# A relaid start: first key cast ahead of the bias table, first query copy on VectorE alone, other spare matmuls, new queue orders

## The chip, the core and the metric

The kernel runs on one core of one Trainium2 chip. The metric is the device time of one execution in microseconds (us), lower is better. PE is TensorE, DVE is VectorE, ACT is ScalarE, POOL is GpSimd, SP is SyncE.

## What is computed

Attention with a relative-position bias over 8 batches and 8 heads, sequence 576, head size 64, followed by a two-layer feed-forward part over 4608 tokens (512 to 2048 to 512):

```python
scores = scale * np.matmul(q, k.transpose(0, 1, 3, 2))
bias = bias_table[bucket]                 # bucket from |i - j|, 32 buckets
scores = scores + bias.transpose(2, 0, 1)[None, :, :, :]
attn = np.exp(scores - max); attn = attn / attn.sum(-1)
out = np.matmul(attn, v)                  # -> x of 4608 x 512
h = x @ w_in;  g = np.maximum(0.01 * h, h);  return g @ w_out
```

Inputs and output are float32; the kernel multiplies in bfloat16.

## The kernel before

The 64 heads are taken as 32 pairs n = 0 to 31, four pairs to a batch. For a pair, queries and keys stand with 96 rows and are turned on PE (`turn_by_pe`, L488 and L493) for the early pairs, by DMA for the later ones; `take_turned` (L502) copies a turned half from PSUM to SBUF, `apart` (L506) makes a copy with the last 64 columns set apart. `score` gives six units u of scores (L527, L531, L534 and L535), each goes through one exponential on ACT (`expo`, L554, L556, L561). The bias is a factor on the exponentials: DVE's `band` (L578) multiplies a band of them by `hk`, which holds exp(bias difference) by distance. Then `av` (L607, L610) multiplies by the values, `norm` divides, and the result is turned into `xT` (L639). The feed-forward part (`ffn_in` L658, `in_product` L706, `product` L783) takes blocks of 512 tokens and runs between the attention of later pairs; it is there from about 34 us to the end.

Before that stands the start-up. The first pair's keys come by an early DMA as float32 into a piece of `y` (called `raw`), and `raw_rows` (L463) casts them to bfloat16 into `pr`, one half on ACT and one on DVE. The first pair's queries come by a POOL DMA. `hk` is made from the 32 x 8 bias table: `some_runs` and `small_runs` (L373, L385, L386) write a one-hot map of distances, `shift_hot` (L394) repeats it shifted, `shift_table` (L399 to L401) turns the table, subtracts its last row and turns it back, `exp_table` (L406) takes exponentials, `spread` (L414, six times) multiplies map by exponentials on PE, `take_spread` (L417) copies that into `hk`, `make_hk4` (L421) copies parts of it. POOL issues all large loads; `clear_v` and `clear_edges` (L325 to L333) are its memsets.

The order of the work on each engine is written out by hand. Every piece is a task with a number, given in the order in which the program adds it; `Plan.QUEUES` lists the numbers for SP, PE, ACT, DVE and POOL, `BANKS` gives the PSUM banks in PE's order, and a copy that either engine can do (`take_turned`, `x_copy`, `in_take`, `out_take`) runs on the engine whose list holds it. `FILL` names PE tasks ahead of which some spare matmuls of constants are put (256 columns, L1284, results unused), and `spin(19)` puts 19 of them ahead of everything.

Of the kernel before, what the change touches and what calls it, by code (L numbers as in the profile page):

```python
# [36 lines left out]
class Plan:  # L37
# [6 lines left out]
            285 335 261 341 393 990 321 399 349 448 989 454 506 376 407 512 561 434 1051 567 462 1050 619 489 520 674  # L44
            625 1156 575 1155 547 602 680 633 660 730 688 732 1257 715 1256 777 738 827 779 765 829 1358 1357 874 785
            835 812 876 1459 882 1458 862 909 1560 1559 1661 1660 1769 1770 1771 1772 1774""",
        "PE": """
# [27 lines left out]
            1749 1744 1754 1755 1752 1753 1757 1758 1763 1764 1765""",  # L75
        "ACT": """
# [17 lines left out]
            1698 1679 1718 1652 1731 1708 1725 1730 1713 1732 1714 1715 1716 1733 1740 1655 1750 1756 1759 1773""",  # L94
        "DVE": """
# [96 lines left out]
def kernel(  # L192
# [10 lines left out]
    nc = tc.nc  # L203
# [57 lines left out]
    RQ = 96  # L261
# [553 lines left out]
    def dma(at):  # L815
        return add("DMA0", 0.0, [], None, 0, at=at)

    L["raw", 0], L["raw", 1], tabl = dma(4.8), dma(3.85), dma(3.0)
    sh = add("DVE", 0.4, [tabl], shift_table, -99)
    e8t = add("ACT", 0.7, [sh], exp_table, -99)  # L820
    hott, shifts = [], []
# [496 lines left out]
```

## Time and profile before

| | |
|---|---|
| median of three runs | 350.75 us (350.03 to 352.52) |
| the profiled execution, own time | 351.14 us |
| its span in the profile | 349.3 us |
| PE, DVE, ACT, POOL busy | 98%, 86%, 82%, 26% of the span |
| exponentials on ACT at L554 | 124, 1033 ns each |
| spare matmuls (L1284) | 34, the last at 23.8 us |

The execution's time is 1.84 us above its span: that lies outside what the engines' records cover. Rows are read as: start, duration (us), engine, line, operation, tiles, shape, count; a bracket gives the idle time of the engine just ahead and what ended it. Overlapping instructions of one row are counted together, so a row's duration can be shorter than the sum of its instructions.

### The profile page before, as it was taken

The page shows a single profiled execution, that of the slowest core. Times are in us where ns is not written, and L with a number is a line of the kernel's source. Part 1 is how long each engine was busy: PE and PEld are TensorE (multiplying, and loading weights), DVE is VectorE, ACT ScalarE, POOL GpSimd, SP SyncE. Part 2 cuts the span into 40 slices and gives each one's busy share as a digit, 9 for nine tenths or more (in the row PEclk, how much of TensorE's full clock was granted, in tenths as well). Part 3 has the DMA queues.
Part 4 walks back from the last instruction along what each step waited for, and adds up shares of the span by engine and source line. Part 5 has one row for each costly group of instructions (what it writes and reads, how often), then busy time and mean ns, then how long its engine had stood idle before and what let it go on. Part 6 is the DMA issues. An engine that isn't in the chain of part 4 may idle for free.

```text
span 349.3 us, 10523 instructions
## 1 busy us (share of the span) xinstructions
PE 343.7 (98%) x4417; PEld 264.5 (76%) x4428; DVE 300.6 (86%) x644; ACT 285.7 (82%) x444; POOL 91.4 (26%) x131
## 2 busy tenths in 40 slices
PE   8999999999999999999999999999999999999996
PEld 5667457774577787778777877787877888888885
DVE  5899399779899999999999989699989995788853
ACT  6899887689889999989989998889968973686641
POOL 8946223053005600794049403200000000000000
PEclk9999999999999999999999999999999999999999
DMA  8999999969959997999569947913940230110033
GB/s 122 153 188 182 197 197 151 132 77 159 172 132 119 141 186 165 73 88 116 178 83 130 121 108 132 127 38 97 152 36 3 85 94 3 75 48 2 0 122 120
DMA packets 118431, 39.32 MB, mean 113 GB/s; under 512 B 100849, under 2 KB 113265, under 8 KB 118385
## 3 DMA queue, kind: packets, MB, share of 16 engines
q0 software_dynamic: 69168, 18.21, 60.0%
q1 hardware_dynamic: 48864, 20.10, 30.2%
q8 instruction: 34, 0.56, 0.7%
q10 hardware_dynamic: 352, 0.36, 0.4%
q14 instruction: 13, 0.10, 0.1%
HBM read 36.70 MB, written 9.44 MB: 132 GB/s over the span
## 4 chain that ended last, share of the span: by engine, by line
PE 95%; DVE 2%; ACT 1%; DMA 1%; issue 0%; DVEq 0%
PE ps L783 32%; PE ps L706 25%; PE ps L607 12%; PE ps L527 10%; PE ps L658 8%; PE ps L534 2%; PE ps L594 1%; PE ps L547 1%; PE ps L493 1%; PE ps L488 1%; PE ps L414 1%; DMA tab<-in_bias_table_dram 1%; PE ps L639 1%; ACT at L554 1%; PE ps L535 0%
## 5 line engine op out<-in xcount | busy, mean ns | idle before, releaser
L554 ACT ACTIVATE at<-ps 128x1024 bf16<-128x1024 f32 x124 | 123.8, 1033 | 15.4 <-PE ps L527 12.7
L783 PEld LDWEIGHTS <-g 128*128 128x128 bf16 x768 | 72.2, 98 | 14.4 <-issue 3.3
L578 DVE TENSOR_TENSOR at<-at,hk 128x768 bf16<-128x768 bf16 (+4 forms) x156 | 65.7, 448 | 10.4 <-ACT at L554 7.0
L313 POOL DMA_DIRECT2D vn<-in_v_dram x32 | 29.7, 940 | 114.4 <-PE ps L607 82.9
L716 DVE TENSOR_TENSOR stage<-ps,stage 128x512 f32<-128x512 f32 x84 | 55.9, 684 | 4.0 <-PE ps L706 1.9
L783 PE MATMUL ps<-mix,g 128*128 128x256 bf16 x384 | 48.2, 273 | 0.0
L706 PEld LDWEIGHTS <-w_in_sb 128*128 128x128 bf16 x448 | 42.4, 98 | 7.5 <-issue 2.4
L783 PE MATMUL ps<-w_out_sb,g 128*128 128x256 bf16 x384 | 47.7, 273 | 0.0
L607 PE MATMUL ps<-vn,at 128*128 128x65 bf16 x1240 | 45.8, 194 | 0.0
L607 PEld LDWEIGHTS <-at 128*128 128x128 bf16 x1240 | 42.2, 97 | 4.6 <-issue 1.7
L647 ACT ACTIVATE g<-stage 128x512 bf16<-128x512 f32 x72 | 42.8, 641 | 1.9 <-DVE stage L716 1.7
L527 PE MATMUL ps<-qkt 64*128 64x512 bf16 x256 | 42.6, 390 | 0.0
L711 ACT COPY stage<-ps 128x512 f32<-128x512 f32 x56 | 31.4, 594 | 12.3 <-PE ps L706 11.2
L706 PEld LDWEIGHTS <-early 128*128 128x128 bf16 x336 | 31.8, 98 | 5.1 <-issue 0.9
L647 ACT ACTIVATE g<-ps 128x512 bf16<-128x512 f32 x56 | 31.7, 608 | 1.4 <-PE ps L658 0.8
L706 PE MATMUL ps<-early,w_in_sb 128*128 128x256 bf16 x224 | 31.2, 273 | 0.0
L706 PE MATMUL ps<-early 128*128 128x256 bf16 x224 | 30.7, 273 | 0.0
L706 PE MATMUL ps<-xT,w_in_sb 128*128 128x256 bf16 x224 | 29.9, 273 | 0.0
L658 PE MATMUL ps<-xT,w_in_sb 128*128 128x512 bf16 x121 | 29.3, 379 | 0.6 <-issue 0.3
L791 ACT COPY y<-ps 128x512 f32<-128x512 f32 x26 | 15.3, 589 | 14.1 <-PE ps L783 12.4
L796 DVE TENSOR_TENSOR y<-ps,y 128x512 f32<-128x512 f32 (+2 forms) x31 | 18.8, 616 | 7.0 <-ACT y L791 4.0
L625 DVE TENSOR_TENSOR opair<-ps,rcp 128x640 bf16<-128x640 f32 x28 | 23.1, 825 | 1.0
(114 smaller groups left out, 494.8 us busy)
## 6 DMA issues: line engine op xcount, KB each, us to landing
out_dram<-y SPq DMA_DIRECT2D x16, 512.0 KB, 3.6
vn<-in_v_dram POOLq DMA_DIRECT2D x32, 128.0 KB, 6.3
qkn<-in_q_dram POOLq DMA_DIRECT2D x10, 288.0 KB, 8.2
qkn<-in_k_dram POOLq DMA_DIRECT2D x10, 288.0 KB, 8.0
w_in_sb<-in_moe_w_in_dram POOLq DMA_DIRECT2D x2, 1024.0 KB, 11.8
w_out_sb<-in_moe_w_out_dram POOLq DMA_DIRECT2D x2, 1024.0 KB, 17.2
qkn<-in_q_dram POOLq DMA_DIRECT2D x16, 72.0 KB, 4.2
qkn<-in_k_dram POOLq DMA_DIRECT2D x16, 72.0 KB, 4.1
```

The source lines that it names most:

```text
L313: nc.gpsimd.dma_start(out=vn[i][:, c, :, 0:D], in_=v[b, :, c * P : (c + 1) * P, :].rearrange("h s d -> s h d"),)
L527: nc.tensor.matmul(ps[:, e, :], lhsT=kt[r, u * P : (u + 1) * P], rhs=qt[r, 0:512], start=True, stop=True)
L554: nc.scalar.activation(at[:, :, u, 0:512], ps, AF.Exp, scale=scale)
L578: nc.vector.tensor_tensor(out=o, in0=o, in1=m, op=ALU.mult)
L607: nc.tensor.matmul(ps[:, ic, :], lhsT=at[:, o : o + P], rhs=vn[i][:, c, 2 * p + e, :], start=whole and c == 0, stop=not whole and ic == NJ ...
L625: nc.vector.tensor_tensor(out=opairs[n % NOP].rearrange("p i (e d) -> p e i d", e=2), in0=ps[:, :, :, 0:D], in1=rcp.to_broadcast([P, 2, NJ ...
L647: nc.scalar.activation(out_, in_, AF.Prelu, bias=0.0, scale=1.0, alpha=0.01)
L658: nc.tensor.matmul(bank(("in", T, f))[:, o : o + n], lhsT=w_in_sb[:, c, f * P : (f + 1) * P], rhs=xT[:, c, x : x + n], start=(c == 0 and i ...
L706: nc.tensor.matmul(ps[:, j, :], lhsT=l, rhs=r, start=first and j == 0 and c == 0, stop=k in (2, 4, 3) and j == 1 and c == KH - 1, skip_gro ...
L711: copy(out=stage[u % 2][:, s], in_=ps)
L716: nc.vector.tensor_tensor(out=st, in0=ps, in1=st, op=ALU.add)
L783: nc.tensor.matmul(ps, lhsT=l[:, ts * P : (ts + 1) * P], rhs=r[:, cols], start=k in (1, 2, 5) and (split or ts == 0) and j == 0, stop=k in ...
```

## The change

Five things are changed.

1. In DVE's list, `small_runs` and `raw_rows` (the key half) stand ahead of `some_runs(2)` and `shift_table`; before, `shift_table` and `small_runs` came first.
2. The first pair's turned queries are copied by one `take_turned` of 576 columns on DVE. Before, ACT copied the first 288 columns and DVE then the other 288. `take_turned` loses its argument `half`. With that ACT copy, one task (number 25) is gone, so every later number is one lower in the new lists.
3. Spare matmuls: 17 instead of 19 ahead of all, and 13 instead of 15 within; five of them now stand ahead of the first `score`.
4. All five lists and the banks are written anew; in PE's list 147 of 662 tasks keep their place, and some 40 copies change between ACT and DVE, about as many each way. In POOL's list `clear_edges` moves from behind the second `clear_v` to just behind the first values' load, that is ahead of the loads of batch 1's queries and keys and of the first half of `w_in`. In SP's list `x_dma(6)` moves ahead of `turn_by_dma(10)`, and others shift by a place.
5. The planner's own guesses (a landing time, a cost) change, which has no effect on the program by itself.

The first tasks on PE and ACT by name (pair n, unit u or half j; j = 1 keys, 0 queries):

```
PE before:  turn(0,k) turn(0,q) spread4 spread5 score(0,1) spread2 score(0,0) spread1 turn(1,k) turn(1,q)
            score(0,2) spread0 score(0,3) turn(2,q) turn(2,k) score(1,1) spread3 score(0,5) [2 spare] score(0,4) ...
PE after:   turn(0,k) turn(0,q) [5 spare] score(0,3) score(0,2) spread5 spread3 spread4 score(0,0) spread1 score(0,1)
            turn(1,k) turn(1,q) score(0,5) spread0 turn(2,q) score(1,1) spread2 score(1,3) turn(2,k) score(1,2)
            score(1,5) [1 spare] score(1,0) [4 spare] turn(3,k) score(0,4) ...
ACT before: some_runs(1) raw_rows exp_table shift_hot(3) take(0,k) take(0,q, half) expo(0,1) expo(0,0) take(1,k) ...
ACT after:  some_runs(1) raw_rows shift_hot(3) take(0,k) exp_table expo(0,3) expo(0,2) expo(0,0) expo(0,1) take(1,q) ...
DVE before: some_runs(0) some_runs(3) shift_table small_runs raw_rows some_runs(2) shift_hot x2 take(0,q, half)
            take_spread4 5 2 1 take(1,q) take_spread0 ...
DVE after:  some_runs(0) some_runs(3) small_runs raw_rows some_runs(2) shift_table shift_hot x2 take(0,q)
            apart x2 take_spread5 4 3 1 take(1,k) apart take_spread0 take(2,q) take_spread2 make_hk4 x2 ...
```

```diff
     QUEUES = {
         "PE": """
-            24 23 41 43 49 37 47 35 71 70 51 33 53 99 100 78 39 57 55 107 80 129 82 86 128 84 113 111 76 109 64 66 105
+            24 23 52 50 42 38 40 46 34 48 70 69 56 32 98 77 36 81 99 79 85 75 128 54 108 112 83 127 110 106 104 65 63
...
         "ACT": """
-            3 22 1 32 27 25 50 48 73 52 54 79 58 56 108 81 83 85 87 114 112 110 77 106 141 139 116 173 137 143 167 145
+            3 22 31 26 1 53 51 47 49 71 57 78 82 80 76 86 55 109 113 84 111 107 105 140 138 115 165 136 134 166 142 144
...
         "DVE": """
-            2 5 0 6 21 4 31 30 26 42 44 38 36 72 34 75 101 28 29 102 40 46 104 74 45 103 131 132 61 90 130 63 59 60 62
+            2 5 6 21 4 0 30 29 25 27 28 43 41 39 35 72 73 33 100 37 44 45 101 60 102 58 62 103 74 130 59 61 91 129 88 89
...
         "POOL": """
-            7 8 9 10 11 13 14 15 12 16 17 18 19 20 273 274 275 388 389 390 501 502 503 614 615 616 727 728 729 824 825
+            7 8 9 10 11 12 13 14 15 16 17 18 19 20 272 273 274 387 388 389 500 501 502 613 614 615 726 727 728 823 824
...
-    FILL = {55: 2, 86: 3, 128: 2, 113: 2, 111: 1, 76: 1, 109: 1, 64: 2, 140: 1}
+    FILL = {52: 5, 75: 1, 128: 4, 112: 1, 110: 1, 104: 1}
...
-    def take_turned(n, j, copy, half=None):
+    def take_turned(n, j, copy):
...
-        rs = slice(0, RQ) if half is None else slice(half * RQ // 2, (half + 1) * RQ // 2)
-        copy(out=turned_to(n, j).rearrange("p (r c) -> p r c", c=NC)[:, rs, :], in_=src[:, rs, :])
+        copy(out=turned_to(n, j).rearrange("p (r c) -> p r c", c=NC), in_=src)
...
-        if n == 0:
-            h = add("ACT", 0.4, [src[0]], lambda: take_turned(0, 0, nc.scalar.copy, 0), feed)
-            cq = add("DVE", 0.06, [src[0], h], lambda: take_turned(0, 0, nc.vector.tensor_copy, 1), feed, give=give[0])
-            ck = add("ACT", 0.53, [src[1]], lambda: take_turned(0, 1, mover(ck)), feed, give=give[1])
...
-    spin(19)
+    spin(17)
     plan.run(spin)
```

More of the change, by code (lines that the diff above doesn't have):

```diff
@@ L43 @@
         "SP": """
-            285 335 261 341 393 990 321 399 349 448 989 454 506 376 407 512 561 434 1051 567 462 1050 619 489 520 674
-            625 1156 575 1155 547 602 680 633 660 730 688 732 1257 715 1256 777 738 827 779 765 829 1358 1357 874 785
-            835 812 876 1459 882 1458 862 909 1560 1559 1661 1660 1769 1770 1771 1772 1774""",
+            284 260 334 340 392 398 989 320 447 348 988 453 505 375 406 511 560 1049 433 461 1050 488 618 566 519 624
+            1154 574 1155 546 673 679 601 632 729 731 659 1256 1255 776 714 687 737 826 778 1356 1357 784 764 828 873
@@ L47 @@
+            811 834 875 861 881 1458 908 1457 1558 1559 1660 1659 1768 1769 1770 1771 1773""",
         "PE": """
[27 rows of a table removed]
-            1749 1744 1754 1755 1752 1753 1757 1758 1763 1764 1765""",
-        "ACT": """
[17 rows of a table removed]
-            1698 1679 1718 1652 1731 1708 1725 1730 1713 1732 1714 1715 1716 1733 1740 1655 1750 1756 1759 1773""",
-        "DVE": """
[23 rows of a table removed]
-            1746 1747 1760 1762 1761 1766 1767 1768""",
[27 rows of a table added]
+            1743 1753 1754 1751 1752 1756 1757 1762 1763 1764""",
+        "ACT": """
[17 rows of a table added]
+            1651 1713 1707 1678 1729 1730 1732 1731 1714 1712 1715 1654 1739 1749 1755 1758 1772""",
@@ L120 @@
+        "DVE": """
[23 rows of a table added]
+            1746 1744 1759 1760 1761 1745 1765 1766 1767""",
         "POOL": """
-            7 8 9 10 11 13 14 15 12 16 17 18 19 20 273 274 275 388 389 390 501 502 503 614 615 616 727 728 729 824 825
-            826""",
+            7 8 9 10 11 12 13 14 15 16 17 18 19 20 272 273 274 387 388 389 500 501 502 613 614 615 726 727 728 823 824
+            825""",
     }
     BANKS = """
-            654605264506245062042604620240630462104624016247102467120642763260437623054364207106742067064732074200244202
@@ L126 @@
-            474102640165462045042610450247624065626046026046020620202602065321420603264106140463260402404060466064310704
-            620342343461466201426442046226426425430623345064064206064302064600462404646041054764306254605640602464104263
-            64244614641647605402602063256043205441037126537640423517647527603231"""
-    FILL = {55: 2, 86: 3, 128: 2, 113: 2, 111: 1, 76: 1, 109: 1, 64: 2, 140: 1}
+            654063246023461204620462402640265042506240526470265476532047205463256204574670426321642014070640210542752024
@@ L131, in __init__ @@
+            402407240732102641321062410321026040340626404624604064040604063107264065460236260304562025622066026206726154
+            025710462476420476420462424002404261207075240276026702026456202626420660260632764065456026210261260241646205
+            42620622606217265142704205432605461440763525630137436571247216345323"""
+    FILL = {52: 5, 75: 1, 128: 4, 112: 1, 110: 1, 104: 1}
     def __init__(self):
@@ L816, in dma @@
         return add("DMA0", 0.0, [], None, 0, at=at)
-    L["raw", 0], L["raw", 1], tabl = dma(4.8), dma(3.85), dma(3.0)
-    sh = add("DVE", 0.4, [tabl], shift_table, -99)
+    L["raw", 0], L["raw", 1], tabl = dma(4.8), dma(3.57), dma(3.75)
+    sh = add("DVE", 0.65, [tabl], shift_table, -99)
     e8t = add("ACT", 0.7, [sh], exp_table, -99)
@@ L921, in plan_rows @@
         behind = ext[n - 1] if n == n_pairs else (sct[n - 2][:1] if n == 2 * n_pairs + 1 else sct[n - 2][1:2] if by_dma(n) else [])
-        if n == 0:
-            h = add("ACT", 0.4, [src[0]], lambda: take_turned(0, 0, nc.scalar.copy, 0), feed)
-            cq = add("DVE", 0.06, [src[0], h], lambda: take_turned(0, 0, nc.vector.tensor_copy, 1), feed, give=give[0])
-            ck = add("ACT", 0.53, [src[1]], lambda: take_turned(0, 1, mover(ck)), feed, give=give[1])
-            ck["other"] = ("DVE", COPYP)
-            cut[0] = [cq, ck] + [add("DVE", 0.14, [t], lambda j=j: apart(0, j), feed + 1) for j, t in ((1, ck), (0, cq))]
-            return
         on_act = n < n_pairs - 1 or n_pairs <= n < 2 * n_pairs
```

128 rows, old and new, of the table QUEUES are left out of this document.

## The prediction

> **What bounds the kernel now.** I read the page first, then PE's idle time, then the first 35 us by windows, chain and timeline.
>
> ```profile
> span 349.3 us, 10523 instructions
> ...
> PE 95%; DVE 2%; ACT 1%; DMA 1%; issue 0%; DVEq 0%
> ```
>
> PE is the chain nearly throughout. A busy PE need not be a useful PE, though, and windows say where it could be otherwise (columns: stretch, its length, then busy us with counts of PE, PE's weight loads, DVE, ACT, POOL):
>
> ```profile
> 5.57:16.30 10.73, 10.71 (x182) 7.31 (x184) 8.07 (x20) 7.81 (x11) 10.13 (x26) 1.00 1.63 148
> 7.33:21.41 14.08, 13.78 (x205) 8.39 (x201) 12.38 (x28) 11.46 (x15) 13.63 (x27) 1.00 1.55 169
> 8.49:21.94 13.45, 13.17 (x188) 7.97 (x188) 11.75 (x27) 11.99 (x15) 12.98 (x26) 1.00 1.56 171
> 21.88:33.60 11.72, 11.62 (x267) 9.27 (x265) 11.07 (x35) 11.72 (x17) 4.30 (x6) 1.00 1.69 174
> 55.50:330.00 274.50, 274.13 (x3503) 216.43 (x3507) 247.77 (x499) 230.32 (x355) 60.35 (x74) 1.00 0.85 101
> ```
>
> From 55.5 to 330 us PE lacks 0.4 us of 274.5: no order of that work gives anything, it can only lose. What can be gained lies ahead of about 34 us, where the feed-forward matmuls begin. The window column of the granted clock says 1.00 throughout, but the same spare matmul (L1284, 256 columns) in three stretches says otherwise (min/median/max ns, first and last start):
>
> ```profile
> L1284 PE MATMUL ps<-const-bfloat16-1.0 x19: 373/421/422, 0.8 to 4.6; 128*128 128x256 bf16 x19
> L1284 PE MATMUL ps<-const-bfloat16-1.0 x2: 401/412/422, 15.3 to 15.5; 128*128 128x256 bf16 x2
> L1284 PE MATMUL ps<-const-bfloat16-1.0 x13: 272/275/285, 17.5 to 23.8; 128*128 128x256 bf16 x13
> ```
>
> PE ran at half pace until about 16 us. The chain through that stretch:
>
> ```profile
> 4.08 0.21 DVE tab_t L399
> ...
> 4.73 0.15 DVE stage L385
> ...
> 4.90 0.21 DVE stage L386
> 5.11 0.42 DVE pr L463
> ...
> 5.57 0.66 PE ps L488 x6
> ...
> 6.86 0.97 PE ps L414 x32
> ...
> 7.84 0.61 PE ps L527 x2
> ```
>
> The table's difference (4.08 to 4.73) and `small_runs` stand ahead of the key cast (to 5.53), the cast ahead of PE; from 5.57 on slow PE itself is the chain. So the start costs by two things: a late cast, and ten microseconds of half-speed PE that feed ACT and DVE slowly.
>
> **The change, part by part.** Timeline rows for it:
>
> ```profile
> 2.76 0.61 DVE L373 COPY stage<-ident 32x6 bf16<-32x6 bf16 x7
> ...
> 3.83 0.51 ACT L463 CAST pr<-y 96x384 bf16<-96x384 f32 x1
> ...
> 4.76 0.86 ACT L406 ACTIVATE diag<-tab 32x8 bf16<-32x8 f32 x4 [0.42 <-DVE tab L401]
> ...
> 4.98 0.53 DVE L463 CAST pr<-y 96x384 bf16<-96x384 f32 x1
> ...
> 5.45 0.39 DVE L373 COPY stage<-ident 32x14 bf16<-32x14 bf16 x4
> ...
> 5.93 0.47 DVE L394 COPY stage<-stage 32x263 bf16<-32x263 bf16 x2
> ...
> 6.36 0.94 ACT L502 COPY qkt<-ps 128x576 bf16<-128x576 bf16 x2
> ...
> 7.33 0.46 DVE L502 COPY qkt<-ps 128x288 bf16<-128x288 bf16 x1 [0.92 <-ACT qkt L502]
> ...
> 8.49 2.11 ACT L554 ACTIVATE at<-ps 128x1024 bf16<-128x1024 f32 x2 [1.19 <-PE ps L527]
> ...
> 11.22 0.76 DVE L502 COPY qkt<-ps 128x576 bf16<-128x576 bf16 x1 [0.42 <-PE ps L493]
> ...
> 12.90 0.21 DVE L506 TENSOR_TENSOR qkt<-qkt,own 128x128 bf16<-128x128 bf16 x1
> ...
> 20.24 0.39 PE L527 MATMUL ps<-qkt 64*128 64x512 bf16 x2
> ```
>
> and from the page a load of 72 KB with its median time from issue to landing:
>
> ```profile
> qkn<-in_q_dram POOLq DMA_DIRECT2D x16, 72.0 KB, 4.2
> ```
>
> *The cast.* DVE ends its seven copies at 3.37, `small_runs` takes 0.38 (4.73 to 5.11) and ends by 3.75; ACT's half of the cast starts at 3.83, when the keys are there, so DVE's can too: 3.83 + 0.53 = 4.36. Both halves then read the same keys at once, which no row shows; one after the other, DVE would end at 4.87, 0.5 later. I take 4.36, as the engines' copies elsewhere overlap. PE turns the keys at about 4.42 instead of 5.57. The spin does not hold it: 19 matmuls start from 0.8 to 4.6, 0.21 us apart, so 17 end near 4.4. With 19 it would have held PE 0.4 us longer.
>
> *The queries.* Key turns 0.66 and query turns take PE to 4.42 + (6.86 − 5.57) = 5.7. The queries' load must have landed: issued at 1.3, median landing 4.2 later, 5.5 at that median; if it holds PE, up to 0.4 of what follows is lost. After 5.8 DVE copies 576 columns at once: 0.76 instead of ACT's part and then 0.46. DVE is free in time: cast to 4.36, `some_runs(2)` 0.39, the table's difference 0.65, shifts 0.47, together 5.87. So the copy goes from about 5.9 to 6.68 (7.79 before), and the first score starts at 6.74 against 7.84. The table's difference, now ending at 5.4, is needed by `exp_table` (0.86 on ACT, now behind the key copy, 5.85 to 6.7): it is hidden under the wait for the query copy, and `spread` comes later than the score now. First exponential: 7.38 instead of 8.49, 1.1 us earlier.
>
> *The spares.* Five ahead of that score take 5 × 0.21 = 1.07, from 5.7 to 6.75: just the wait for DVE's copy, so nothing if the copy ends at 6.68. But PE is now unbroken from 0.8 to past 7.8 (spin, turns, spares, two scores), 7 us. Before, a 0.6 us hole followed the spin, and after it short spreads and mode changes left holes until the clock rose at about 16. I take it that the clock rises within that stretch, by 7.8. What it does for PE between 5.57 and 16.3: six scores fall from 0.61 to 0.39 busy (1.3), sixty turning matmuls from the first of these rates to the second (groups by form ahead of and behind the clock's rise: count, busy us and mean ns, idle us ahead):
>
> ```profile
> L493 PE MATMUL ps<-ident,qkn 96*64 96x96 bf16 x60 | 3.0, 282 | 0.0
> ```
>
> ```profile
> L493 PE MATMUL ps<-ident,qkn 96*64 96x96 bf16 x48 | 1.8, 210 | 0.0
> ```
>
> The turns fall from 0.050 to 0.038 us each, 0.7; the two score units with other shapes are put at 0.2 each from the same ratio: about 2.4 us less PE, and PE stops being what ACT and DVE wait for.
>
> *The Trainium skill on this.* "TensorE: Matmul & The Clock Gate", section "What's actually happening", says that the clock is opened by activity over a window of some 3.4 us that runs freely of the kernel. By it a stretch of 7 us holds a whole window wherever it lies, and the spin of 4.2 us need not: the trace, in which the spin did not raise the clock, agrees. It speaks for 7.8 us as the latest time; and it speaks against any saving from the two spares taken out, since they ran in a stretch where they cost PE nothing.
>
> *What is late next: DVE or ACT.* ACT's large exponentials between the first of them and the first `av`:
>
> ```profile
> L554 ACT ACTIVATE at<-ps 128x1024 bf16<-128x1024 f32 x7 | 7.1, 1027 | 2.3 <-PE ps L527 2.2
> ```
>
> The idle time ahead of them (1.2 of it ahead of the first) was for slow scores. In that stretch ACT is idle 13.45 − 11.99 = 1.46 us; starting 1.1 earlier it could gain up to 2.6. DVE is busy 12.38 of the 14.08 us from its first copy to the last band that the first `av` needs (21.41), idle 1.7. Now it starts at 5.9 instead of 7.33 and has 0.30 more (0.76 for 0.46). Its idle time doesn't vanish: after the copy and two `apart` (to 6.95) it needs the first spread, which stands behind two scores: 6.74 + 0.54 + 0.32 + 0.43 and 0.2 to land, about 8.25, so 1.3 idle, and 0.1 more later. End: 5.9 + 12.38 + 0.30 + 1.4 = 20.0: 1.4 earlier. Between 21.9 and 33.6 DVE has 0.65 idle and ACT none; one early copy more goes to ACT, one x copy to ACT from DVE. So I take DVE's 1.4 and half of its 0.65: **1.7 us gained** at the feed-forward part, between 1.4 and ACT's 2.6. PE, dense from there, keeps it.
>
> *What moves behind.* POOL's six edge memsets ahead of three loads, one of them `w_in`'s first half, cost 0.6 us of issue at most (the queue was some 7 us ahead of that half's first use, below). SP has `x_dma(6)` ahead of `turn_by_dma(10)`:
>
> ```profile
> 33.66 0.81 PE L658 MATMUL ps<-xT,w_in_sb 128*128 128x512 bf16 x2
> ...
> 69.51 1.20 SPq L631 DMA_TRANSPOSE xT<-opair  x1
> ...
> 94.83 0.38 PE L534 MATMUL ps<-qkt 128*128 128x512 bf16 x1
> ```
>
> The turn of pair 10 then waits for pair 6's output, which is issued at 69.51; pair 10's first score stands at 94.83, so even ten places earlier in the new list it is covered. Against `w_out`, whose second half lands last, stand (its landing times, then its issue, DVE's last mix and PE's first product):
>
> ```profile
> DMA to landing us min/median/max: 15.2/17.2/19.2
> ```
>
> ```profile
> 30.83 0.92 POOL L438 DMA_DIRECT2D w_out_sb<-in_moe_w_out_dram  x1 [0.50 <-DMA vn<-in_v_dram]
> ...
> 54.53 0.69 DVE L732 TENSOR_TENSOR mix<-w_out_sb,mix 128x1024 bf16<-128x1024 bf16 x1
> ...
> 55.51 0.71 PE L783 MATMUL ps<-w_out_sb,g 128*128 128x256 bf16 x5
> ```
>
> The slower half, issued at 30.83, is there at 30.83 + 19.2 = 50.0; four mixes of 0.69 follow, so products that need them can start at 52.8, and the first stood at 55.51. The loads allow 2.7 us; 1.7 fits. SP's other places shift by one and move nothing past a wait that ends later than this one.
>
> The copies exchanged between ACT and DVE later cost nothing as long as neither is late (DVE 90%, ACT 84% in the long window): between nothing and a few tenths, I take nothing.
>
> **Sum.** 351.14 − 1.7 = 349.4 for the profiled execution; its own time is 0.4 above the median of the runs shown, so 350.75 − 1.7, rounded to 349.0.
>
> **The rivals.**
>
> *All of it kept.* DVE is not late (its list puts bands of pair 0 first, a copy and a band less ahead of `av`), and ACT sets the start: −2.6, 348.15. For it: ACT is busy for all of 21.88 to 33.6. Against: DVE's 12.38 of 14.08. If neither held, PE's own share (1.1 earlier and 2.4 less) would give 350.75 − 3.5 = 347.25.
>
> *The clock stays down to 16 us.* Then PE remains the chain: its unbroken work begins at 6.74 instead of 6.79, and ahead of pair 3's turn it has five spares (1 + 4) where it had two: +3 × 0.21 = 0.6, slower: 351.35. It decides if a hole in the early stretch is too long, say the cast or the queries late by 0.5. For it: PE looked busy for 10.71 of 10.73 us from 5.57 on, and stayed slow.
>
> *Given back later.* The relaid lists meet waits that before had none (the window of 274 us can only lose), or `w_out` lands later: the 1.7 shrink to nothing, 350.7. Same time if the cast isn't earlier, because the keys land late in a usual execution.
>
> **How the numbers follow.** Chances: forecast 0.55 (own range 348.5 to 349.6), all kept 0.18, clock down 0.12, given back 0.15. The range, 347.4 to 351.2, leaves out some of the outer ends. About 1% (3.5 us) is what a measurement of this kernel can tell from no change. Faster by more (under 347.2) needs more than any engine's share above: 0.08; slower by more 0.03; within 0.89.
>
> **What would show it.** Right: key turns (L488) at 4.4; the first L554 near 7.4; spare matmuls ahead of 8 us falling to 0.27; the first L607 near 20 or before; first L658 near 32. Wrong: the spares at 20 us still the first fast ones; DVE or ACT with new idle time after 55 us; PE's window of 55 to 330 lacking over 1 us.

## The result, and the profile after

The changed kernel ran at a median of 348.82 us (348.48 to 350.12, 10 runs) beside 350.83 us (349.65 to 352.52, 10 runs) for the kernel before: a ratio of 0.9943 [0.9924, 0.9962], 2.0 us less, under the 1% that was named. The forecast was 349.0 us. The profiled execution took 350.12 us, 1.3 above its kernel's median; why is read below. Behind `take_turned` line numbers are one lower in the kernel after (the score's L527 is L526, the first `av` L606, the feed-forward part L657); the spares' L1284, further down, is L1275.

The first stretch, from the timeline of the profiled execution (start us, duration, engine, line, operation, count, and in a bracket the idle time ahead and what ended it):

```profile
3.80 0.51 ACT L463 CAST pr<-y 96x384 bf16<-96x384 f32 x1
3.80 0.55 DVE L463 CAST pr<-y 96x384 bf16<-96x384 f32 x1
...
4.40 0.45 PE L488 MATMUL ps<-ident,pr 96*128 96x96 bf16 x6
...
5.15 0.45 PE L493 MATMUL ps<-ident,qkn 96*64 96x96 bf16 x12 [0.29 <-DMA qkn<-in_q_dram]
...
5.41 0.61 DVE L394 COPY stage<-stage 32x263 bf16<-32x263 bf16 x2
...
5.53 0.73 PE L1275 MATMUL ps<-const-bfloat16-1.0 128*128 128x256 bf16 x5
...
6.06 0.76 DVE L501 COPY qkt<-ps 128x576 bf16<-128x576 bf16 x1
...
6.87 0.61 PE L526 MATMUL ps<-qkt 64*128 64x512 bf16 x4 [0.61 <-ACT diag L406]
...
7.30 1.94 ACT L553 ACTIVATE at<-ps 128x1024 bf16<-128x1024 f32 x2 [0.46 <-PE ps L526]
...
13.40 1.96 DVE L421 COPY hk<-hk 64x768 bf16<-64x768 bf16 x2
...
20.09 0.30 PE L606 MATMUL ps<-vn,at 128*128 128x65 bf16 x4
```

Both halves of the cast read the keys at once and lose next to nothing (0.51 and 0.55 us, where they took 0.51 and 0.53 one after the other). The keys turn at 4.40 (5.57 before), the first score stands at 6.87 (7.84), the first exponential at 7.30 (8.49). The bracket at the score names `exp_table` on ACT, but that does not feed a score; what the score needs is the query copy, 6.06 to 6.82. And that copy came not when PE had turned the queries but when DVE had ended its two shifts, at 6.02.

The five spares are all fast, which says that PE's clock was up by 5.5 us in this execution (minimum, median, maximum ns):

```profile
L1275 PE MATMUL ps<-const-bfloat16-1.0 x5: 274/275/285, 5.5 to 6.0; 128*128 128x256 bf16 x5
```

Later, in windows (stretch, its length, then busy us and counts of PE, PE's weight loads, DVE, ACT, POOL, then granted clock, DMA share, GB/s):

```profile
5.57:16.30 10.73, 8.90 (x181) 6.02 (x181) 9.52 (x18) 10.23 (x16) 10.11 (x25) 1.00 1.61 144
...
53.60:329.00 275.40, 274.46 (x3504) 217.18 (x3503) 250.11 (x503) 229.99 (x355) 57.30 (x73) 1.00 0.81 101
```

PE's load between 5.57 and 16.3 fell from 10.71 to 8.90 us. The long window lacks 0.94 us, where before it lacked 0.4. The chain and the waits give the place:

```profile
78.49 14.14 DMA tu<-pr
```

```profile
PE ps L526 <- DVE opair L624: 0.8, 1, 0.8
```

```profile
DVE pr L458 <- DMA tu<-pr: 1.8, 1, 1.8
```

A DMA turn (issued at 78.49, there only at 92.63; what made it so late was not followed up) held a copy on DVE for 1.8 us; a division queued behind it on DVE came late, and a score on PE waited 0.8 us for that. In the trace of before, no DVE instruction behind 34 us waits for a DMA.

A second execution of the same kernel (after_2, below; 348.29 us, span 346.3) has neither that wait nor the slow pair of `make_hk4` copies at 13.40 us (1.23 us in place of 1.96):

```profile
13.40 1.23 DVE L421 COPY hk<-hk 64x768 bf16<-64x768 bf16 x2
...
19.34 0.30 PE L606 MATMUL ps<-vn,at 128*128 128x65 bf16 x4
...
30.48 0.81 PE L657 MATMUL ps<-xT,w_in_sb 128*128 128x512 bf16 x3
```

```profile
53.60:329.00 275.40, 275.28 (x3513) 218.01 (x3512) 250.51 (x503) 230.90 (x357) 57.72 (x74) 1.00 0.85 101
```

Where the time came from, then, in this execution beside the profiled one of before: the feed-forward part begins at 30.48 instead of 33.66, 3.18 earlier, and of that 3.0 reaches the end (346.3 against 349.3).

### The profile page after: what moved, and what is told of

The parts are those of the page before. It is cut to its first block, busy times and chain, and to the rows that moved or that the text cites. A ratio compares the mean times of both kernels' runs of the same rounds, so it can differ in the third digit from the quotient of the medians.

```text
span 348.1 us, 10539 instructions
## 1 busy us (share of the span) xinstructions
PE 341.0 (98%) x4424; PEld 263.8 (76%) x4424; DVE 303.7 (87%) x646; ACT 284.3 (82%) x441; POOL 88.7 (25%) x131
## 4 chain that ended last, share of the span: by engine, by line
PE 83%; DVE 8%; DMA 6%; issue 1%; ACT 0%; POOL 0%; DVEq 0%; POOLq 0%; ACTq 0%
PE ps L782 30%; PE ps L705 23%; PE ps L606 11%; PE ps L526 8%; DMA tu<-pr 6%; PE ps L657 4%; PE ps L533 2%; DVE at L577 1%; DVE qkt L501 1%; PE ps L593 1%; PE ps L546 1%; DVE stage L715 1%; DVE hk L417 1%; PE ps L638 1%; PE ps L488 1%
## 5 line engine op out<-in xcount | busy, mean ns | idle before, releaser
L782 PE MATMUL ps<-w_out_sb,g 128*128 128x256 bf16 x384 | 46.6, 273 | 0.0
L606 PEld LDWEIGHTS <-at 128*128 128x128 bf16 x1240 | 42.3, 98 | 4.6 <-issue 2.5
L606 PE MATMUL ps<-vn,at 128*128 128x65 bf16 x1240 | 45.6, 194 | 0.0
L526 PE MATMUL ps<-qkt 64*128 64x512 bf16 x256 | 42.2, 382 | 1.6 <-DVE opair L624 0.8
L710 ACT COPY stage<-ps 128x512 f32<-128x512 f32 x50 | 28.5, 599 | 10.6 <-PE ps L705 9.1
L790 ACT COPY y<-ps 128x512 f32<-128x512 f32 x29 | 17.1, 590 | 19.6 <-PE ps L782 19.6
L705 PE MATMUL ps<-early,w_in_sb 128*128 128x256 bf16 x224 | 32.4, 273 | 0.0
L705 PE MATMUL ps<-xT,w_in_sb 128*128 128x256 bf16 x224 | 31.5, 273 | 0.0
L657 PE MATMUL ps<-xT,w_in_sb 128*128 128x512 bf16 x128 | 29.8, 380 | 0.0
L710 DVE COPY stage<-ps 128x512 f32<-128x512 f32 x34 | 22.9, 686 | 6.4 <-PE ps L705 5.7
## 6 DMA issues: line engine op xcount, KB each, us to landing
w_in_sb<-in_moe_w_in_dram POOLq DMA_DIRECT2D x2, 1024.0 KB, 10.7
```

The lines of the kernel that those rows point to most:

```text
L526: nc.tensor.matmul(ps[:, e, :], lhsT=kt[r, u * P : (u + 1) * P], rhs=qt[r, 0:512], start=True, stop=True)
L606: nc.tensor.matmul(ps[:, ic, :], lhsT=at[:, o : o + P], rhs=vn[i][:, c, 2 * p + e, :], start=whole and c == 0, stop=not whole and ic == NJ ...
L657: nc.tensor.matmul(bank(("in", T, f))[:, o : o + n], lhsT=w_in_sb[:, c, f * P : (f + 1) * P], rhs=xT[:, c, x : x + n], start=(c == 0 and i ...
L705: nc.tensor.matmul(ps[:, j, :], lhsT=l, rhs=r, start=first and j == 0 and c == 0, stop=k in (2, 4, 3) and j == 1 and c == KH - 1, skip_gro ...
L710: copy(out=stage[u % 2][:, s], in_=ps)
L782: nc.tensor.matmul(ps, lhsT=l[:, ts * P : (ts + 1) * P], rhs=r[:, cols], start=k in (1, 2, 5) and (split or ts == 0) and j == 0, stop=k in ...
```

## The experiments

The theory: the gain is the clock, up some ten microseconds earlier, plus an earlier first score. The rivals: one of the two does it alone; VectorE's load hides one of them; PE's new waits give it back. The kernel before ran at 351.6 us (349.55 to 352.99, 23 runs) beside the first four kernels, 351.64 (350.43 to 352.87, 13 runs) beside the next four and 350.99 (349.66 to 352.3, 23 runs) beside the last four. Each ratio is to that. "Clock up" is the time of the first rise in the trace's record of the granted clock.

The record also has the mean granted clock of every execution. One stretch of 3.41 us at 0.50 takes 0.005 off the mean of a span of 347 us: the trace of a_no5_again, which has one such stretch, reads 0.995. By that, 38 of the 59 executions of the kernel before beside these experiments had one to three such stretches behind the first rise (means of 0.995 to 0.984), and none of the 29 executions of the kernel after had one (0.999 or 1.000). So in most executions of before the clock does not just rise late, as in the profiled one: it rises and falls again. The mean leaves out the slow time ahead of the first rise; the profiled execution of before, slow up to 16.34 us, reads 1.000.

**after_again**: the kernel after, unaltered.

> The changed kernel once more, unaltered, for its own profile beside the others. The profile at hand has TensorE's clock up at 4.5 us and a wait of 1.0 us at 94.7 us that its ten runs' median (1.3 us below the profiled one) may not have. If that wait belongs to one execution: median 348.8 and no TensorE wait over 0.3 us behind 31 us; if it is the order's: the wait is there again.

348.95 us (348.38 to 349.22), ratio 0.9927 [0.9905, 0.995]: 2.65 below before. Clock up at 5.38, score 6.88, `av` 19.57. The wait at 94 us is not there: the order does not bring it in every execution.

**b_spin22**: the kernel before, with three more spares ahead of all.

```diff
-    spin(19)
+    spin(22)
```

> The kernel before with 22 instead of 19 spare matmuls ahead of all, which fills the hole from 5.0 to 5.5 us ahead of the key turns and moves nothing else. Theory (half of the gain is the clock): the clock is up by 7.6 us in nearly all runs, TensorE no longer holds VectorE and ScalarE back, and the time falls by 0.8 to 1.4 us to 349.4 to 350.0. Rival (the earlier cast and the new order gain all): 350.8, unchanged, whatever the clock does.

350.06 us (349.63 to 352.66), ratio 0.9965 [0.9946, 0.9985]: 1.54 below before, by the clock alone, since the score stays at 7.84. The clock was up at 3.56 us in the profiled execution, where before's stood at 16.34. The hole was not filled as expected: with the clock up the spares ended at 4.70, and PE then stood idle for 0.87 us until the key turns. At 3.56 the 19 spares of before would still have been running, too, so here the three more did not bring the rise. What they do shows in the mean granted clock, which is 0.999 or more in 11 of 12 executions, against 8 of 23 of before: the clock stays up. The first `av` is as early as that of after (19.50), but the feed-forward part begins at 32.26, so the first `av` alone does not tell the end.

**a_cold**: the kernel after without the spares (one is left).

```diff
-    FILL = {52: 5, 75: 1, 128: 4, 112: 1, 110: 1, 104: 1}
+    FILL = {}
...
-    spin(17)
+    spin(1)
```

> The changed kernel with one spare matmul in place of 17 and none of the 13 within: TensorE is idle until the key turns at 4.4 us and again until the first score. Theory: the clock comes up some 10 us later, the first av at 21.5 us or later instead of 20.1, and the time is 350.3 to 351.2. Rival (order and cast gain all, spares cost something): 348.8 or less.

350.98 us (349.58 to 353.41), ratio 0.999 [0.9965, 1.0016]: no difference from before that shows, 2.03 above after_again. The score stands at 6.87 as in after, but the clock was up only at 12.98, and the scores say so:

```profile
L526 PE MATMUL ps<-qkt x8: 579/606/631, 6.9 to 10.3; 64*128 64x512 bf16 x8
```

In after_again the same matmuls have a median of 387 ns from 6.9 to 12.5. So the clock is worth some 2.0 us in this order. (The profiled execution took 352.70, 1.7 above the median; it also lost to late DMA turns behind 34 us, 1.7 us of waits on DVE, and is read here only up to 13 us.) By the differences (clock alone 1.54, the rest without clock 0.62, both 2.65), the two help each other somewhat, though 0.5 is within what these medians can be off.

**a_table**: the kernel after, with the bias table's difference back ahead of the key cast (and 22 spares, meant to leave no hole; in the trace 0.68 us are left ahead of the key turns).

```diff
-            2 5 6 21 4 0 30 29 25 27 28 43 ...
+            2 5 0 6 21 4 30 29 25 27 28 43 ...
...
-    spin(17)
+    spin(22)
```

> The changed kernel with the bias table's difference ahead of the key cast again on VectorE (shift_table before small_runs and raw_rows), and 22 spare matmuls ahead so that TensorE stays unbroken. Theory: key turns at about 5.1 instead of 4.4 us, first exponential about 0.7 later, clock as in the changed kernel: 0.4 to 0.8 us slower, 349.2 to 349.6. Rival (VectorE has slack, the cast is not what sets the start): 348.8.

349.34 us (348.57 to 349.9), ratio 0.9939 [0.9916, 0.9963]. The keys turn at 5.58, 1.2 later than in after_again and 0.5 later than expected, but the score only 0.39 later, at 7.27, since the table's work, done ahead, no longer stands between the cast and the shifts. The time is 0.39 above after_again; the intervals overlap, and in its trace the feed-forward part begins no later (30.83 against 31.00), so that this is the expected size and not shown. By the medians the earlier cast is the smallest of the three parts.

**after_2**: the kernel after again, as the partner of the next three.

> The changed kernel unaltered, as the measure for the three beside it on this chip: 348.8 to 349.0, highest less than 1 us above lowest (the profiled one of the first series apart).

348.76 us (348.2 to 350.48), ratio 0.9933 [0.9906, 0.9959]. Highest and lowest are 2.3 apart, where less than 1 was expected.

**a_half**: the first queries copied in two halves again, by ACT and then DVE.

```diff
-                 lambda: take_turned(n, 0, mover(cq)), ...
+                 lambda: take_turned(n, 0, mover(cq)) if n else (take_turned(0, 0, nc.scalar.copy, 0),
+                         take_turned(0, 0, nc.vector.tensor_copy, 1)), ...
```

> The changed kernel with the first query copy in two halves again, ScalarE's and then VectorE's. The halves take 0.40 and 0.46 one after the other where the whole takes 0.76, and ScalarE's exp_table comes 0.4 later: first score at 7.0 instead of 6.88, first exponential 7.4 to 7.7 instead of 7.31. Theory: 348.9 to 349.3, hardly to be told from the changed kernel. Rival (the copy on VectorE alone carries what cast and clock leave unexplained): 349.6 or more.

349.91 us (349.28 to 350.67), ratio 0.9951 [0.9934, 0.9968]: 1.15 above after_2, more than expected, though the intervals overlap. ACT's half fell behind `exp_table` in ACT's order:

```profile
6.88 0.40 ACT L502 COPY qkt<-ps 128x288 bf16<-128x288 bf16 x1
...
7.31 0.46 DVE L502 COPY qkt<-ps 128x288 bf16<-128x288 bf16 x1 [1.27 <-ACT qkt L502]
...
7.82 0.39 PE L527 MATMUL ps<-qkt 64*128 64x512 bf16 x2 [1.10 <-DVE qkt L502]
```

The first score stands 0.95 later than in after_2, and in the two traces, both with the clock up, the feed-forward part begins 0.97 later (31.45 against 30.48). Three of the eight executions also lost a stretch of the clock (mean 0.995); the other five have a median of 349.61, 0.85 above after_2. By these figures, that DVE copies alone is the bigger part of the earlier score: it takes ACT, with `exp_table` on it, out of the way. ACT's half ahead of `exp_table` was not tried.

**a_no5** and, on another chip, **a_no5_again**: the kernel after without the five spares ahead of the first score.

```diff
-    FILL = {52: 5, 75: 1, 128: 4, 112: 1, 110: 1, 104: 1}
+    FILL = {75: 1, 128: 4, 112: 1, 110: 1, 104: 1}
```

> The changed kernel without the five spare matmuls ahead of the first score; the 17 ahead and the other 8 stay. TensorE is then unbroken from 0.8 to 5.6 us only, with a hole of about 1.2 us behind. Theory (a whole window of some 3.4 us of unbroken work raises the clock, wherever the windows lie): about half of the runs have the clock up by 5.6 and take 348.9, the others get it some microseconds later and take up to 350.9; median 349.0 to 350.2, lowest and highest over 1.5 apart. Rival (the five only sit in a wait): 348.9, lowest and highest less than 1 apart.

349.6 us (349.29 to 349.95), ratio 0.9944 [0.9925, 0.9962]: 0.84 above after_2. The median is as the theory had it, the spread of 0.66 as the rival had it; in its profile the clock rose at 5.78 and stayed, so the cause was open.

> The kernel after without the five spares ahead of the first score, a second time, since its 0.8 above the kernel after came with a trace that was the same on PE up to 29 us. Theory (the five spares cost and save nothing once the clock is up, and the 0.8 is the spread between executions): within 0.3 of after_3. Rival (the hole of 1.1 us ahead of the score lets the clock fall or rise late in many executions): again 0.6 to 1.0 above after_3, and the profile shows matmuls of the first spread or turns at half pace.

349.7 us (348.65 to 350.05), ratio 0.9957 [0.9939, 0.9976]: 0.61 above after_3. Here the profile shows the rival at work. Windows cut at the changes of the clock:

```profile
4.05:7.46 3.41, 1.79 (x27) 0.88 (x25) 2.87 (x13) 2.16 (x8) 3.26 (x8) 1.00 1.10 135
7.46:10.87 3.41, 3.41 (x82) 2.46 (x82) 2.58 (x4) 3.14 (x4) 3.11 (x5) 0.50 1.34 167
10.87:14.28 3.41, 3.41 (x85) 2.35 (x80) 3.13 (x6) 3.25 (x5) 3.41 (x11) 1.00 2.23 139
```

```profile
6.88 0.61 PE L526 MATMUL ps<-qkt 64*128 64x512 bf16 x4 [1.40 <-ACT diag L406]
...
8.81 0.61 PE L526 MATMUL ps<-qkt 64*128 64x512 bf16 x2
...
9.89 0.61 PE L526 MATMUL ps<-qkt 64*128 64x512 bf16 x2
```

The number behind the five busy times is the granted clock: 1.00, 0.50, 1.00. The clock had risen at 4.05; in the next 3.41 us PE worked 1.79, with a hole of 1.4 ahead of the score; then the clock was halved for the next 3.41, and each pair of score matmuls at 8.81 and 9.89 took 0.61 instead of 0.39. In the first a_no5 the stretch with the hole began at the hole (5.78) and held more work, and the clock stayed:

```profile
5.78:9.19 3.41, 2.31 (x60) 1.72 (x61) 2.33 (x7) 2.89 (x8) 2.96 (x7) 1.00 1.14 151
```

The five spares thus are not needed to raise the clock; they keep it up through DVE's copy. The traces show this in one execution of two, and the mean granted clock tells how often. It is 0.995, one stretch lost, in 8 of 10 executions of a_no5_again (349.40 to 350.05 us; the two at 1.000 took 348.65 and 348.99), and in 3 of 6 of a_no5. It is below 0.999 in 3 of 8 of a_half and in 8 of 10 of a_nofill as well. The traces of these four kernels have a hole of 1.1 to 1.4 us ahead of the first score. Where spares stand ahead of the score and the trace's hole is 0.61 us at most (after, a_hk4, a_copyfirst, a_table), none of 46 executions lost a stretch. So a hole above 1 us ahead of the score goes with a lost stretch in many executions; where the stretch lay, only the one trace shows. It is not all of the 0.84: the three executions of a_no5 that kept the clock took 349.29 to 349.56, and what holds them above after_2 stays open. The medians agree in sign on both chips, but their intervals overlap those of the kernel after.

**a_hk4**: a query copy that PE waits for at 15 us moved ahead of the two `make_hk4` copies on DVE.

```diff
-            ... 37 44 45 101 60 ...
+            ... 37 101 44 45 60 ...
```

> The changed kernel with the third pair's key copy ahead of the two make_hk4 copies on VectorE. TensorE's wait of 0.7 to 1.2 us at 15 us for the bank that this copy frees goes away. Theory (VectorE's whole work sets the end of the start-up, not TensorE): first av within 0.3 us of the changed kernel's, 348.6 to 349.0. Rival (TensorE's wait is on the path): 348.0 to 348.4.

348.85 us (348.43 to 348.95), ratio 0.9922 [0.9903, 0.994], as after_2. PE's wait at 15 us (0.45 in after_2, 1.19 in the first profile) is gone, and nothing came of it: in that stretch DVE's whole work counts, not the place at which PE waits for it.

**after_3**: the kernel after, as the partner of the last three.

> The kernel after, unaltered, beside the three below on one chip. By what was measured so far it takes 348.7 to 349.1, some 2.6 to 2.9 below the kernel before. Theory (the gain is the clock plus an earlier first score; the rest of the spread between executions comes from short copies on VectorE that take different times beside POOL's work): first score again within 6.85 to 6.9, clock up between 4 and 6.5 us, first av between 19.3 and 20.1, and the pair of make_hk4 copies (L421) takes more time where av is later. Rival (the spread is the clock, which rises at another moment): av is later where the clock rises later.

349.09 us (348.69 to 350.18), ratio 0.9947 [0.9924, 0.997]. Clock up at 5.37 as in after_again, but the first `av` 0.56 later; and the `make_hk4` copies took that much more:

```profile
13.43 1.99 DVE L421 COPY hk<-hk 64x768 bf16<-64x768 bf16 x2
...
20.13 0.30 PE L606 MATMUL ps<-vn,at 128*128 128x65 bf16 x4
```

In the four traces of this kernel, the two copies (their durations added: 1.93, 1.41, 1.19, 1.96 us) and the first `av` (20.09, 19.57, 19.34, 20.13) differ by 18.16, 18.16, 18.15 and 18.17. The clock (up at 4.49, 5.38, 6.11 and 5.37) shows no such relation. For the first `av` the rival is out.

**a_copyfirst**: one of DVE's two shifts moved behind the query copy, four spares for five.

```diff
-            2 5 6 21 4 0 30 29 25 27 28 43 ...
+            2 5 6 21 4 0 30 25 29 27 28 43 ...
...
-    FILL = {52: 5, 75: 1, ...
+    FILL = {52: 4, 75: 1, ...
```

> The kernel after with one of VectorE's two shift copies of the one-hot map (about 0.3 us) moved behind the copy of the first queries, and four spares instead of five. The queries' turn ends near 5.75 while VectorE's shifts end at 6.03 to 6.06, so the query copy can start some 0.3 earlier. Theory (an earlier first score is worth about 1 us per us): copy at 5.77, first score near 6.6 instead of 6.87, first exponential near 7.03, time 0.25 below after_3. Rival (what is late behind it, the first spread, is no earlier, and VectorE's work up to the first av is the same sum): first score 6.6, but av and the end where they are in after_3, within 0.1.

348.8 us (348.23 to 349.0), ratio 0.9932 [0.9902, 0.9961]: 0.29 below after_3. In its timeline (line numbers 23 lower):

```profile
5.85 0.76 DVE L478 COPY qkt<-ps 128x576 bf16<-128x576 bf16 x1
...
6.66 0.61 PE L503 MATMUL ps<-qkt 64*128 64x512 bf16 x4 [0.46 <-DVE qkt L478]
...
7.09 3.78 ACT L530 ACTIVATE at<-ps 128x1024 bf16<-128x1024 f32 x4 [0.25 <-PE ps L503]
...
7.20 1.37 PE L391 MATMUL ps<-diag,stage 128*128 128x32 bf16 x48
```

Everything in this stretch, the first spread too (7.43 in after_3), stands 0.23 earlier, and the first `av` at 19.06 is the earliest of all runs (less the two `make_hk4` copies' 1.11: 17.95, where the kernel after has 18.16); against the rival, the time follows. But the intervals overlap: a better order by some 0.25 us, likely and not proved.

**a_nofill**: the 17 spares ahead of all kept, none of the thirteen later ones.

```diff
-    FILL = {52: 5, 75: 1, 128: 4, 112: 1, 110: 1, 104: 1}
+    FILL = {}
```

> The kernel after with its 17 spares ahead of all, but none of the twelve later ones. Theory (the clock is up by then through the spin and the turns, and later spares lie in PE's waiting time): clock up at 4 to 6.5 us, time within 0.3 of after_3; where a quarter or more of the executions have the clock up only near 13 us, the median is up to 2 above. Rival (the spares hold the clock up in the early stretch): clock granted below full for part of 7 to 16 us, the first av about 1 later, time 1 to 2 above after_3.

349.66 us (349.16 to 350.81), ratio 0.9959 [0.9941, 0.9977]: 0.57 above after_3, between both expectations. The clock rose at 6.03 and stayed, the first `av` stands at 19.34, so this execution lost nothing early. It lost at 71 us, where DVE was again held by a DMA turn:

```profile
PE ps L606 <- DVE at L577: 0.9, 1, 0.9
```

```profile
DVE pr L458 <- DMA tu<-pr: 1.1, 1, 1.1
```

Its other executions did lose by the clock, as a_no5's do: the mean granted clock is 0.995 or 0.994 in five (one stretch) and 0.990 in three (two stretches), and these three are the slowest (350.38 to 350.81). No execution of a_no5 or a_no5_again lost two, so the eight other spares may hold the clock up somewhere too; no trace shows where.

## Why the prediction was right

- **Cast.** Forecast 4.42 for the key turns, measured 4.36 to 4.45 in four executions. The doubt whether both halves can read at once is settled (0.55 and 0.51, both from 3.80). The queries' load did hold PE, for 0.29, and that cost nothing, since DVE's shifts ended later.
- **First score.** Forecast 6.74, measured 6.87; first exponential 7.38 against 7.30. The shifts were put at 0.47 and took 0.61, which a_copyfirst suggests to matter. That the exponential comes out as close is luck in part: it was put 0.64 behind the score, the distance at half pace, and stands 0.43 behind it, which makes up for the later score. The five spares cost nothing, as said; but the reason to have them was underrated: a_no5_again shows what they hold.
- **Clock.** "By 7.8" held: 4.5 to 6.1 us in four executions. In three of them it came from the spares at the start plus the turns, ahead of the five; in after_2 it rose while the five ran, but a_nofill, without them, has it at 6.03. What kept it down in before was given as holes behind the spin's; the row from 5.57 to 16.30 has PE idle for 0.02 us, so holes are not the reason there (see the last section). In a_no5_again the changes at 4.05, 7.46 and 10.87 us are twice 3.41 apart. The Trainium skill, "TensorE: Matmul & The Clock Gate", section "What's actually happening", gives a free-running window of 3413 ns. The distances agree with it. That section of the Trainium skill also puts the return to half speed behind an idle window. Here a window with 1.79 us of work in 3.41 was enough, and the measurement decides.
- **What is late next.** DVE, as forecast: the first `av` moves with the time of its `make_hk4` copies. Its idle time ahead of the first spread was forecast at 1.3 and is 0.93 in all four executions. It has 12.11 us of work from the copy to the first `av` in after_2 and 12.86 in the first profile (12.85 before, by the same count); the windows read:

```profile
6.06:19.34 13.28, 12.30 (x220) 7.87 (x219) 12.11 (x27) 12.79 (x21) 12.37 (x28) 1.00 1.52 152
19.34:30.48 11.14, 11.12 (x263) 9.17 (x262) 10.75 (x34) 10.98 (x16) 5.41 (x8) 1.00 1.74 176
```

```profile
6.06:20.09 14.03, 11.97 (x218) 7.64 (x217) 12.86 (x27) 12.91 (x21) 13.12 (x28) 1.00 1.53 159
```

```profile
7.33:21.88 14.55, 14.25 (x207) 8.61 (x204) 12.85 (x29) 11.93 (x15) 13.85 (x27) 1.00 1.53 170
```

  The first two rows are after_2, the third is the first profile of the kernel after, the last the kernel before. **This is the term that was mis-sized.** The sum took DVE's load as unchanged plus 0.30, that is 12.68 to the last band ahead of the first `av`. By the same count it is 11.39 in after_2 (6.06 to 18.62, 26 instructions instead of 28): one `take_turned` and one `apart` fewer stand ahead of that band, and one of the six bands has 192 columns in place of 768. The rival "all kept" had supposed a copy and a band less; the copy is right. Part of the fall, some 0.3, is not the new list's: b_spin22, with DVE's list of before, has 12.05 by this count (7.33 to 19.57), where the slow trace gave 12.38. So `av` came 2.54 earlier in after_2, not 1.4. In the two executions with slow `make_hk4` copies the load is higher by their time and `av` came 1.8 earlier, which is why the forecast fits them better.
- **From `av` to the feed-forward part.** Forecast: half of 0.65 gained. Measured: 0.64 in after_2 (11.78 to 11.14 us), 0.35 in after_again, 0.62 and 0.57 in the other two.
- **PE, dense from there, keeps it.** From the first feed-forward matmul to the end of the span: 315.6 us before, 315.8 to 316.1 in the three later executions of after, 316.9 in the first. A little was given back in each, and 1 more where DVE was held by the DMA turn. That is a small part of the rival "given back later", through a new wait and not through `w_out`. Whether the new order of SP's list makes that wait was not tried.
- **The size.** Forecast 1.7 off 350.75; measured 2.0 in that series, and 2.65, 2.88 and 1.90 in the other three, where the kernel before stood at 351.6, 351.64 and 350.99. The forecast lay at the low end: the start gave more than forecast (the feed-forward part begins 2.3 to 3.2 earlier in the four executions, not 1.7), and the later part gave some back. That the two partly cancel is luck. The sum was also worked out on one execution of before in which the clock rose once, late, while in most it rose and fell again; that its time lies near the others' median is luck too.
- **"The clock stays down"** was put at 351.35, slower than before. a_cold comes near that case, though its clock is up at 12.98 and not at 16, and it lacks the three spares that the rival charges 0.6 for. It is level with before at 350.98 (beside 351.6): the earlier score is worth little to a slow PE.

## What to carry to other kernels

Ahead of a dense main part, look at the time that one repeated instruction takes, not at PE's busy share: 10.7 busy microseconds of 10.73 hid a clock worth some 2 us. Cheap spare matmuls paid here where they filled a stretch of 3.4 us without a hole, and again, by the granted clock and less surely by the times, where they covered a wait of more than 1 us shortly after. One trace tells little of a clock that differs between executions: compare the mean granted clock of all runs. When a start is pulled in by reordering, take the next engine's load up to the target from the new order, not from the old trace.

## What was not expected of the hardware

- **Busy is not enough for the clock.** Two of the 3.41 us stretches of before, counted back from its rise at 16.34, look full, and did not raise it:

```profile
6.10:9.51 3.41, 3.39 (x67) 2.28 (x66) 2.42 (x6) 2.19 (x4) 2.96 (x7) 1.00 1.15 163
9.51:12.92 3.41, 3.41 (x68) 2.35 (x68) 2.29 (x5) 2.77 (x5) 3.41 (x6) 1.00 1.94 143
```

  They hold turns, spreads of 32 columns and scores on 64 rows; which of these does not count was not tried. In a_no5_again a stretch of the same three kinds did raise it. To keep a clock that is up, far less was enough: the first profile of the kernel after holds 2.16 us of work from 14.73 to 18.14, three stretches behind its rise at 4.49, and the clock stayed, while 1.79 us in a_no5_again did not keep it. The column of the granted clock says 1.00 in the two rows above although PE ran at half pace; it shows a low clock only behind the first rise.
- **DVE's copies from SBUF to SBUF vary.** The `make_hk4` copy of 64 x 768 took 340 to 1237 ns over the runs, and the first `av` of the kernel after moved by the same amount. POOL issues loads beside it (13.05 to 15.2 us), but at the same moments in the executions with slow copies and in the others. The Trainium skill, "SBUF — State Buffer", section "SBUF: two separate sides", describes a port pair that DVE and GpSimd hold by turns for a whole instruction. It could make such differences; no run here takes POOL's work away, so the cause stays open.
